# Gated delta attention and MLP on one core: keys and queries turned by VectorE and DMAs instead of TensorE

## The chip, the core and the metric

The kernel runs on one core of a Trainium2 chip. A core has TensorE (PE; PEld is its weight load), VectorE (DVE), ScalarE (ACT), GpSimd (POOL) and SyncE (SP), each with an instruction queue of its own that is worked off in order. Transfers are issued from the queues of SP and ScalarE. The metric is the device time of one execution in microseconds (us); less is better.

## What is computed

Cut from the reference: a delta-rule recurrence over 768 tokens in 32 heads (4 in the batch, 8 heads each, head size 48), and on its output an MLP with a hardswish.

```python
q, k, v: (4, 8, 768, 48); beta: (4, 8, 768); w_in: (384, 2048); w_out: (2048, 384)

k_n = k / (np.linalg.norm(k, axis=-1, keepdims=True) + 1e-06)
for t in range(S):
    y[:, :, t] = einsum('bhd,bhde->bhe', q[:, :, t], state)
    v_old = einsum('bhde,bhd->bhe', state, kt)
    state = state + bt[:, :, :, None] * einsum('bhd,bhe->bhde', kt, vt - v_old)
x = y.transpose(0, 2, 1, 3).reshape(3072, 384)
h = x @ w_in
out = (h * np.clip(h + 3.0, 0.0, 6.0) / 6.0) @ w_out
```

All is in float32.

## The kernel before

**Chunks and steps.** The 768 tokens of a sequence are cut into N = 24 chunks of C = 32. The 128 partitions of a tile hold 4 batch entries x 32 tokens of a chunk. Step t runs the chain of chunk t, and in the profile it begins with the product of keys and queries with the state (L806). A chunk needs, ahead of its step:

- `prep(t)`: GpSimd scales the keys to unit length (`kb`, L510); TensorE transposes keys and then queries, four 128x128 transposes each into a PSUM tile `pt` (L524); ScalarE copies each `pt` into a quarter of the tile `KQ`, which holds keys and queries with the head dimension on the partitions (L532); GpSimd makes a mask (`mb`, L486); TensorE multiplies keys with keys and queries (the scores `sc`, L547); VectorE masks these into `L` and `LB` (L558); GpSimd scales the keys by beta (`bkb`, L498).
- `inverse(g)`: for a group of four chunks (5 to 8, 9 to 12, 13 to 16, 17 to 20, 21 to 23) VectorE inverts the unit triangular matrices `L`, 30 rounds of a product (L759) and a difference (L764), between two block transposes of 128x1024 (L469, L473). The inverse of the next group is worked off during the present one, in pieces.

`chain(t)`, in order: L806 on TensorE; `R` from the values and the product with the state (L901, L909 on VectorE); `y` from the product with the queries (L843 on ScalarE, then L819 on VectorE); `pz`, the inverse times `R` (L827), which ScalarE copies out (L927); the new state (L938 on TensorE, L956 on VectorE); `py` (L827), added to `y` (L863); `y` transposed for the MLP (L873, copied by L877).

**MLP.** Two chunks make a block of 256 tokens. From block 5 on the up product is made by a scheme with eleven products instead of twelve: VectorE first makes sums of the tokens (`token_sums`, L1056); then for each of eight tiles TensorE begins (`begin`, L1066), ScalarE copies the first half of it (L1080), GpSimd forms sums (L1030), TensorE ends it (`end`), VectorE adds (L1093, L1097), ScalarE copies the rest, which empties the PSUM buffer (L1100), and makes the clipped part (L1104), and VectorE multiplies (L1107). Before block 5 the plain product stands there (L994, L1001 on ScalarE, L1004 on VectorE). From block 2 on the down product is made with seven half-size products (L1218); its sums are L1204 and L1228, ScalarE's copies L1225. The down product of one block runs in odd steps, the up product of the next in even steps. The result goes out from SP (`to_dram`, L1143): eight transfers of 48 KB near the end of each odd step.

**Order.** Every engine's order is written by hand. Up to step 4 a string lists each piece of work. From step LS = 5 on a loop has NU = 15 units a step. `plan` says which generator is advanced in which unit: `ch` is the chain, `now` the `prep` of the chunk whose products are made next, `later` the one after it; from step 7 on `now` is chunk t + 6. In every unit one piece of the MLP follows (`take(units)`), then pieces of the inverse, as many as a running sum allows (`room`, from constants for what VectorE has to do in that unit):

```python
room = max(1.65 - USED[mode["of"]] - CHAIN.get(u, 0), 0.15) / mode["mean"]
due += room * left / max((GS - i) * NU - u, 1)
```

In the kernel before, from step 7 on, `prep` scales the keys in unit 13, transposes keys in unit 1 of the next step and queries in unit 2, makes the scores in unit 4 and the masks in unit 5. The inverse starts in unit 6 of the second step of a group. `prep` of the last chunk, 23, ends in step 17.

**Buffers.** PSUM has a ring `pm` of four buffers, shared by `pt`, `pz`, `py`, the transposed `y` and the tiles of the MLP, and a ring `pc` of two for the state's products and the scores. `KQ` has six buffers, keys two (`kb`), queries four (`qb`). A query or key transfer has rows of 48 numbers (192 bytes), 256 rows in each.

Of the kernel before, what the change touches and what calls it, by code (L numbers as in the profile page):

```python
# [9 lines left out]
FP32 = mybir.dt.float32  # L10
# [34 lines left out]
def kernel(  # L45
# [34 lines left out]
    CB = 2  # L80
# [36 lines left out]
    mb_spare = spares[:, 8 * H * C : 10 * H * C]  # L117
    bkb_spare = spares[:, 10 * H * C : 10 * H * C + H * DP].rearrange("p (h w) -> p h w", w=DP)
    assert 10 * H * C + H * DP == 3 * NPR * P
    kbufs = [persist.tile([P, H, DP], FP32, name=f"kb{i}") for i in range(NKB)]  # L120
    qbufs = [persist.tile([P, H, DP], FP32, name=f"qb{i}") for i in range(NQB)]
    bkbufs = [bkb_spare] + [
        persist.tile([P, H, DP], FP32, name=f"bkb{i}") for i in range(1, NBKB)
    ]
# [12 lines left out]
    def needs(*what):  # L137
        assert past.issuperset(what), (what, set(what) - past)
# [33 lines left out]

    def load_q(t, eng=nc.sync):
        if t < N:
            if t >= NQB:
                needs(("qT", t - NQB))
            elif t:
                needs(*pad(t))
            for b in range(B):
                eng.dma_start(out=qbufs[t % NQB][rows(b), :, 0:D], in_=tokens(q, b, t))  # L180
                if b == B - 1:
                    past.add(("q", t))
                yield
# [310 lines left out]
    def scaled(t):  # L494
        needs(("kb", t), *pad(t), *([("bkb", t - NKB)] if t >= NKB else []))
        if t >= NBKB:
            needs(("su", t - NBKB + 1))
        nc.gpsimd.tensor_tensor(  # L498
            out=bkb_of(t)[:, :, 0:D], in0=kbufs[t % NKB][:, :, 0:D],
            in1=beta_tok[:, t, 0:H].unsqueeze(2).to_broadcast([P, H, D]), op=ALU.mult,  # L500
        )
        past.add(("bkb", t))
        yield

    def prep(t, whole=True):

        g, i = group(t)
        kb, qb = kbufs[t % NKB], qbufs[t % NQB]
        needs(*([("bkb", t - NKB)] if t >= NKB else []), *(pad(t) if t < NKB and t else []))
        nc.gpsimd.tensor_tensor(  # L510
            out=kb[:, :, 0:D], in0=kfs[g][:, i],
            in1=invs.pop(t).unsqueeze(2).to_broadcast([P, H, D]), op=ALU.mult,
        )
        past.add(("kb", t))
        yield

        for j, src in enumerate((kb, qb)):
            if j == 1:
                needs(("q", t))
                past.add(("qT", t))  # L520
            ring("pm", NPM, ("pt", t, j))
            pt = psM.tile([128, NP, P], FP32, name="pt", tag=slot["pm"])
            for p in range(NP):
                nc.tensor.transpose(  # L524
                    pt[:, p, :], src[:, 2 * p : 2 * p + 2].rearrange("p e w -> p (e w)"), ident[:]
                )
# [12 lines left out]
        ring("pc", NPC, ("sc", t))  # L539
        sc = psC.tile([P, 2, 512], FP32, name="sc", tag=slot["pc"])  # L540
        scv = sc[:, :, 0 : NP * 2 * C].rearrange("p e (a j w) -> p e a j w", a=NP, j=2)
        for p in range(NP):
            for b in range(B):
                for e in range(2):
                    r = slice(DP * e, DP * e + DP)
                    kq = KQ[r, p * B // 2 + b // 2]
                    nc.tensor.matmul(  # L547
                        scv[rows(b), e, p],
                        lhsT=kq[:, 3 if b % 2 else 0, :],
                        rhs=kq[:, 3:1:-1, :] if b % 2 else kq[:, 0:2, :],  # L550
                        start=True, stop=True,
                    )
        yield
        needs(*([("BZ", t - NLB)] if t >= NLB else []))
        LB = work.tile([P, H, C], FP32, name="LB", bufs=NLB)
        mb = mbs.pop(t)
        for j, out in enumerate((lowers(t), LB)):
# [229 lines left out]
    def chain(t, whole=True):  # L787
# [10 lines left out]
        def of_state():  # L798
            ph = [banks("ks", t, i) for i in range(2)]
            for p in range(NP):  # L800
                for b in (0, 2, 1, 3):
                    for e in range(2):
                        r = slice(DP * e, DP * e + DP)
# [622 lines left out]
    with tc.manual_schedule():  # L1426
# [11 lines left out]
        loads = iter(())  # L1438
        left = due = 0
        USED = {"up": 0.42, "eleven": 1.0, "down": 0.7}  # L1440
        CHAIN = {0: 0.45, 1: 0.75, 2: 0.75, 3: 0.4, 4: 0.4, 6: 0.5, 9: 0.8, 10: 0.6, 14: 0.2}
        for t in range(LS, N):
            g, i = group(t)
# [9 lines left out]
            if i == 2:  # L1453
# [12 lines left out]
                11: lambda: token_sums(t // CB),  # L1466
                13: lambda: take(later),
            }
            if behind:
                for u in (7, 8, 10, 11, 12, 13):  # L1470
                    plan[u] = lambda ch=plan.get(u): (ch and u < 13 and ch(), take(more))
                plan[14] = lambda: take(later)
            ready = (2, 0) if behind or i == 2 and t - LS == LA - LE else (1, 6)
            for u in range(NU):
                if u in plan:
                    plan[u]()
# [13 lines left out]
                settle(1)  # L1490
                while evicts:
                    evicts.pop(0)()
                if i == 1 == ready[0] and 5 < u < 7:
                    continue
                if i == 0 or not left:
                    take(fill, 2 if i or u < 2 else u > 4)
                    continue
                room = max(1.65 - USED[mode["of"]] - CHAIN.get(u, 0), 0.15) / mode["mean"]
                due += room * left / max((GS - i) * NU - u, 1)
                due = min(due, 2.6)  # L1500
                take(fill, int(due))
# [34 lines left out]
```

## Time and profile before

| | us |
|---|---|
| runs shown: median of 3 (lowest to highest) | 667.09 (667.01 to 669.37) |
| profiled execution | 672.08 |
| its span, first to last instruction | 670.4 |
| TensorE busy in the span | 636.9 |
| VectorE busy | 487.2 |
| ScalarE busy | 272.8 |
| GpSimd busy | 203.6 |

The granted clock of TensorE is 0.985 on average over the span, and 1.00 in every stretch from 130 us on. The profile is of one execution; a row gives line, engine, operation, tiles (out<-in) and shapes, count, busy time and the mean of one in ns, and then idle time of the engine just before it with what ended it. "SPq" and "ACTq" are transfers issued on these queues; "to landing" is the time from issue until the semaphore says that the data is there. Some steps: step 7 begins at 214.8 us, step 12 at 342.2, step 16 at 443.3, step 17 at 468.3, step 18 at 493.4.

### The profile page before, as it was taken

To read this page: it belongs to the slowest core of one execution; us is meant where nothing else is said; L and a number is where in the kernel's file an instruction comes from. 1 tells how busy PE (TensorE), PEld (TensorE's weight loads), DVE (VectorE), ACT (ScalarE), POOL (GpSimd) and SP (SyncE) were. 2 spreads that over 40 slices of the span, in tenths; PEclk is the share of its full clock that TensorE was granted. 3 is DMA by queue.
4 is the path that set the end of the run, shared out by engine and by line. 5 is a ranking of instruction groups with operands and counts; after the bars stand their busy time and mean duration, and the time that the engine had idled before them with its cause. 6 is when DMAs were issued, how large, how long until landed. Compare 5 with 4: busy or idle time off the path is not lost.

```text
span 670.4 us, 26330 instructions
## 1 busy us (share of the span) xinstructions
PE 636.9 (95%) x11544; PEld 568.6 (85%) x11544; DVE 487.2 (73%) x1146; ACT 272.8 (41%) x532; POOL 203.6 (30%) x320
## 2 busy tenths in 40 slices
PE   2768899999999999999999999999999999999997
PEld 2657786776688988988989999999999999999997
DVE  4889685899545777747879847988748988556354
ACT  5887568532142232232234234235244144153250
POOL 5531022002421031364155255055042141331330
PEclk9959899999999999999999999999999999999999
DMA  7888237302041030032030020020020020010000
GB/s 171 203 193 235 59 67 186 73 6 51 15 80 32 2 72 2 3 73 37 3 68 8 3 61 14 3 62 2 3 50 2 2 49 2 17 24 2 25 1 25
DMA packets 88499, 33.27 MB, mean 50 GB/s; under 512 B 80160, under 2 KB 83232, under 8 KB 88384
## 3 DMA queue, kind: packets, MB, share of 16 engines
q1 hardware_dynamic: 88128, 31.29, 20.7%
q8 instruction: 91, 1.49, 0.9%
q10 hardware_dynamic: 256, 0.30, 0.2%
q14 instruction: 24, 0.20, 0.1%
HBM read 26.84 MB, written 4.72 MB: 47 GB/s over the span
## 4 chain that ended last, share of the span: by engine, by line
PE 86%; DMA 5%; DVE 3%; SPq 2%; issue 1%; ACT 1%; POOL 0%; ACTq 0%; DVEq 0%; POOLq 0%
PE po L1218 28%; PE ph L1066 20%; PE ph L994 15%; PE po L1154 6%; PE ks L806 3%; PE su L938 3%; PE pz L827 3%; PE py L827 3%; PE pt L524 2%; PE sc L547 2%; DMA spare<-in_moe_w_in_dram 2%; DMA kf<-in_k_dram 1%; PE yt L873 1%; DMA w_out<-in_moe_w_in_dram 1%; PE pi L684 1%
## 5 line engine op out<-in xcount | busy, mean ns | idle before, releaser
L1066 PE MATMUL ph<-xT,w_in 128*128 128x128 f32 (+1 forms) x560 | 121.4, 321 | 0.8 <-ACT KQ L532 0.6
L994 PE MATMUL ph<-xT,w_in 128*128 128x256 f32 (+1 forms) x576 | 116.6, 351 | 2.9 <-DVE g L1004 2.1
L1218 PE MATMUL po<-w_out,g 128*128 128x192 f32 x640 | 110.6, 326 | 0.0
L994 PEld LDWEIGHTS ph<-xT,w_in 128*128 128x128 f32 x576 | 94.5, 192 | 15.8 <-DVE g L1004 2.9
L1218 PEld LDWEIGHTS po<-w_out,g 128*128 128x128 f32 x640 | 104.6, 190 | 0.5
L1066 PEld LDWEIGHTS ph<-xT,w_in 128*128 128x128 f32 x560 | 91.1, 191 | 6.0 <-ACT KQ L532 0.8
L1030 POOL TENSOR_TENSOR g<-g 128x256 f32<-128x256 f32 x112 | 68.0, 608 | 83.2 <-ACT g L1080 78.8
L1218 PE MATMUL po<-spare,g 128*128 128x192 f32 x480 | 86.7, 332 | 0.0
L1218 PEld LDWEIGHTS po<-spare,g 128*128 128x128 f32 x480 | 77.2, 190 | 1.8
L1001 ACT ACTIVATE g<-ph,halves 128x256 f32<-128x256 f32 (+1 forms) x96 | 41.3, 436 | 74.9 <-PE ph L994 74.8
L1080 ACT ACTIVATE g<-ph 128x512 f32<-128x512 f32 x56 | 33.4, 597 | 82.1 <-PE ph L1066 82.1
L1228 POOL TENSOR_TENSOR o<-o,u 128x192 f32<-128x192 f32 x18 | 13.2, 733 | 175.7 <-ACT o L1225 97.2
L1204 DVE TENSOR_TENSOR g<-g 128x512 f32<-128x512 f32 x80 | 55.6, 716 | 5.6 <-PE po L1218 5.6
L759 DVE TENSOR_TENSOR pr<-A 128x30 f32<-128x30 f32 (+9 forms) x150 | 57.4, 383 | 2.8
L764 DVE TENSOR_TENSOR A<-A,pr 128x30 f32<-128x30 f32 (+9 forms) x150 | 55.7, 371 | 3.7
L1004 DVE SCALAR_TENSOR_TENSOR g<-g,ph 128x256 f32<-128x256 f32 (+1 forms) x96 | 34.8, 371 | 31.7 <-ACT g L1001 31.4
L356 ACT ACTIVATE spare<-spare,places 128x768 uint16<-128x768 uint16 (+1 forms) x56 | 52.4, 942 | 2.7 <-DMA kf<-in_k_dram 1.5
L1093 DVE TENSOR_TENSOR g<-ph,g 128x256 f32<-128x256 f32 x56 | 23.5, 420 | 38.4 <-PE ph L1066 30.9
L1225 ACT ACTIVATE o<-po 128x192 f32<-128x192 f32 x40 | 13.2, 330 | 83.2 <-PE po L1218 79.6
L510 POOL TENSOR_TENSOR kb<-kf,inv 128x384 f32<-128x384 f32 x24 | 21.3, 891 | 78.8 <-issue 42.6
L1154 PE MATMUL po<-w_out,g 128*128 128x384 f32 x128 | 45.2, 491 | 0.0
L1107 DVE SCALAR_TENSOR_TENSOR g<-o,g 128x512 f32<-128x512 f32 x56 | 40.7, 726 | 5.9 <-ACT o L1104 5.9
(141 smaller groups left out, 1010.6 us busy)
## 6 DMA issues: line engine op xcount, KB each, us to landing
kf<-in_k_dram SPq DMA_DIRECT2D x96, 48.0 KB, 2.9
qb<-in_q_dram SPq DMA_DIRECT2D x96, 48.0 KB, 2.8
vf<-in_v_dram SPq DMA_DIRECT2D x96, 48.0 KB, 2.2
out_dram<-o SPq DMA_DIRECT2D x92, 48.0 KB, 1.6
spare<-in_moe_w_in_dram SPq DMA_DIRECT2D x4, 768.0 KB, 6.0
w_out<-in_moe_w_in_dram SPq DMA_DIRECT2D x4, 768.0 KB, 6.5
w_out<-in_moe_w_out_dram SPq DMA_DIRECT2D x4, 768.0 KB, 7.3
spare<-in_moe_w_out_dram SPq DMA_DIRECT2D x4, 768.0 KB, 5.7
```

The costliest lines, as they stand in the source:

```text
L356: nc.scalar.activation(out=z, in_=z if n else d.bitcast(I16)[:, :, :, 3], func=func, bias=places[:, n : n + 1], scale=scale,)
L759: nc.vector.tensor_tensor(out=pv, in0=A[:, j + 1 :, j].unsqueeze(2).to_broadcast([n, w, j]), in1=A[:, j, 0:j].unsqueeze(1).to_broadcast([n ...
L764: nc.vector.tensor_tensor(out=A[:, j + 1 :, 0:j], in0=A[:, j + 1 :, 0:j], in1=pv, op=ALU.subtract)
L827: nc.tensor.matmul(ps[rows(place(b)), D * h : D * h + D], lhsT=m(h)[rows(b)], rhs=z[rows(b), D * at(h) : D * at(h) + D], start=True, stop= ...
L994: nc.tensor.matmul(ph[:, cols], lhsT=w_in[:, s, f * 128 : (f + 1) * 128], rhs=xT[:, s, cols], start=(s == 0), stop=(s == NKT - 1),)
L1001: nc.scalar.activation(out=g, in_=ph, func=ACTF.Relu, bias=half, scale=1.0 / 6.0)
L1030: nc.gpsimd.tensor_tensor(out=out, in0=a, in1=b, op=op)
L1066: nc.tensor.matmul(ph[:, n], lhsT=w, rhs=x, start=start, stop=stop, skip_group_check=True)
L1107: nc.vector.scalar_tensor_tensor(out=g, in0=r, scalar=1.0, in1=g, op0=ALU.min, op1=ALU.mult)
L1154: nc.tensor.matmul(pos[c][:], lhsT=gs[blk, f // 2][:, f % 2, c * P : (c + 1) * P], rhs=w_out[:, f, :], start=(f == 0), stop=(f == NFC - 1),)
L1204: nc.vector.tensor_tensor(out=A(f, *out, 4), in0=A(f, *a, 4), in1=A(f, *b, 4), op=op)
L1218: nc.tensor.matmul(ps[n][:], lhsT=A(f - f % 2, *a)[:, f % 2], rhs=b[:, f], start=(f == 0), stop=(f == HF - 1),)
```

## The change

For chunks t >= TQ = 13 (prepared in steps 7 to 17) `prep` has no TensorE transposes and no ScalarE copies. VectorE turns the scaled keys, and then the queries, in blocks of 32x32 (one 128x384 instruction each) into `turned`, which lies in two of the former four query buffers. SP writes each half with four transfers into a DRAM tile `kq`, in rows of 32 numbers. When all eight are there, ScalarE issues two transfers that read `kq` into `KQ`. Scores and the products with the state then use 48 rows per head instead of 64. Keys and queries of these chunks are stored densely, and queries have two buffers.

The plan changes for these chunks: keys are scaled in unit 10, turned with their four writes in unit 11, queries with theirs in unit 12, the reads in unit 1 of the next step, scores in unit 6, masks in unit 7. The inverse starts in unit 8 instead of 6, and its pace leaves room for the turning in units 11 and 12.

```diff
+    TQ, HQ = LS + 2 * LE, 2
+    qb_pair = persist.tile([P, HQ, H, DP], FP32, name="qbs")
...
+    turned = qb_pair[:].rearrange("p i h w -> p (i h w)")[:, 0 : 2 * H * D].rearrange(
+        "p (k z) -> p k z", k=2
+    )
...
-        for j, src in enumerate((kb, qb)):
+        if t >= TQ:
+            kq = scratch.tile([H * D, B // 2, 4, C], FP32, name="kq", bufs=2)
+            for j, src in enumerate((of_key(t), of_query(t))):
+                if j == 1:
+                    needs(("q", t))
+                    past.add(("qT", t))
+                nc.vector.transpose(out=turned[:, j], in_=src.rearrange("p h w -> p (h w)"))
+                for b in range(B):
+                    nc.sync.dma_start(
+                        out=kq[:, b // 2, (3 if j == 0 else 2) if b % 2 else j, :].rearrange(
+                            "(n r) c -> r n c", r=C
+                        ),
+                        in_=turned[rows(b), j].rearrange("p (n c) -> p n c", c=C),
+                    )
+                yield
+            ring("KQ", NKQ, ("KQ", t))
+            KQ = work.tile([128, NP * B // 2, 4, C], FP32, name="KQ", bufs=NKQ)
+            for e in range(2):
+                nc.scalar.dma_start(
+                    out=KQ[DP * e : DP * e + D].rearrange("d (p x) y c -> d p (x y c)", p=NP),
+                    in_=kq[:].rearrange("(p e d) x y c -> e d p (x y c)", e=2, d=D)[e],
+                )
+            drain(mask(t))
+            yield
+        for j, src in enumerate((kb, qb) if t < TQ else ()):
...
+        TURN = {11: 0.75, 12: 0.75}
...
+            if first_of >= TQ:
+                plan[2] = lambda: (take(ch), take(gens["q"], 4))
+                plan[4] = lambda: take(ch)
+                plan[5] = lambda: None
+                plan[7] = lambda: take(now)
+            if first_of + 1 >= TQ and not behind:
+                plan[10] = lambda: (take(ch), take(later))
+                plan[11] = lambda: (token_sums(t // CB), take(later))
+                plan[12] = lambda: take(later)
+                plan[13] = lambda: None
...
-            ready = (2, 0) if behind or i == 2 and t - LS == LA - LE else (1, 6)
+            turns = TURN if first_of + 1 >= TQ else {}
+            by_dma = first_of >= TQ
+            ready = (2, 0) if behind or i == 2 and t - LS == LA - LE else (1, 8 if by_dma else 6)
...
-                room = max(1.65 - USED[mode["of"]] - CHAIN.get(u, 0), 0.15) / mode["mean"]
+                room = max(1.65 - USED[mode["of"]] - CHAIN.get({6: 7, 8: 6}.get(u, u) if by_dma else u, 0) - turns.get(u, 0), 0.15) / mode["mean"]
```

More of the change, by code (lines that the diff above doesn't have):

```diff
@@ L119, with of_key, of_query, dense @@
     assert 10 * H * C + H * DP == 3 * NPR * P
-    kbufs = [persist.tile([P, H, DP], FP32, name=f"kb{i}") for i in range(NKB)]
-    qbufs = [persist.tile([P, H, DP], FP32, name=f"qb{i}") for i in range(NQB)]
+    kbufs = [persist.tile([P, H, DP], FP32, name=f"kb{i}")[:] for i in range(NKB)]
+    TQ, HQ = LS + 2 * LE, 2
+    qb_pair = persist.tile([P, HQ, H, DP], FP32, name="qbs")
+    qbufs = [persist.tile([P, H, DP], FP32, name=f"qb{i}")[:] for i in range(NQB - HQ)] + [
+        qb_pair[:, i] for i in range(HQ)
+    ]
+    turned = qb_pair[:].rearrange("p i h w -> p (i h w)")[:, 0 : 2 * H * D].rearrange(
+        "p (k z) -> p k z", k=2
+    )
+    def of_key(t):
+        return dense(kbufs[t % NKB], t)
+    def of_query(t):
+        return dense(qbufs[t % NQB if t < TQ else t % (NQB - HQ)], t)
+    def dense(x, t):
+        if t < TQ:
+            return x[:, :, 0:D]
+        return x.rearrange("p h w -> p (h w)")[:, 0 : H * D].rearrange("p (h w) -> p h w", w=D)
+    def q_before(t):
+        slot = [s % NQB if s < TQ else s % (NQB - HQ) for s in range(t + 1)]
+        return max((s for s in range(t) if slot[s] == slot[t]), default=None)
     bkbufs = [bkb_spare] + [
@@ L174, in load_q @@
         if t < N:
-            if t >= NQB:
-                needs(("qT", t - NQB))
+            if q_before(t) is not None:
+                needs(("qT", q_before(t)))
             elif t:
@@ L179, in load_q @@
             for b in range(B):
-                eng.dma_start(out=qbufs[t % NQB][rows(b), :, 0:D], in_=tokens(q, b, t))
+                eng.dma_start(out=of_query(t)[rows(b)], in_=tokens(q, b, t))
                 if b == B - 1:
@@ L498, in scaled @@
         nc.gpsimd.tensor_tensor(
-            out=bkb_of(t)[:, :, 0:D], in0=kbufs[t % NKB][:, :, 0:D],
+            out=bkb_of(t)[:, :, 0:D], in0=of_key(t),
             in1=beta_tok[:, t, 0:H].unsqueeze(2).to_broadcast([P, H, D]), op=ALU.mult,
@@ L510, in prep @@
         nc.gpsimd.tensor_tensor(
-            out=kb[:, :, 0:D], in0=kfs[g][:, i],
+            out=of_key(t), in0=kfs[g][:, i],
             in1=invs.pop(t).unsqueeze(2).to_broadcast([P, H, D]), op=ALU.mult,
@@ L544, in prep @@
                 for e in range(2):
-                    r = slice(DP * e, DP * e + DP)
+                    r = slice(DP * e, DP * e + (DP if t < TQ else D))
                     kq = KQ[r, p * B // 2 + b // 2]
@@ L802, in of_state @@
                     for e in range(2):
-                        r = slice(DP * e, DP * e + DP)
+                        r = slice(DP * e, DP * e + (DP if t < TQ else D))
                         c = slice(2 * C * (b // 2), 2 * C * (b // 2) + 2 * C)
@@ L1472 @@
                 plan[14] = lambda: take(later)
-            ready = (2, 0) if behind or i == 2 and t - LS == LA - LE else (1, 6)
+                if first_of + 2 == TQ:
+                    plan[12] = plan[13] = lambda: (take(more), take(later))
+            turns = TURN if first_of + 1 >= TQ else {}
+            by_dma = first_of >= TQ
+            ready = (2, 0) if behind or i == 2 and t - LS == LA - LE else (1, 8 if by_dma else 6)
             for u in range(NU):
@@ L1492 @@
                     evicts.pop(0)()
-                if i == 1 == ready[0] and 5 < u < 7:
+                if i == 1 == ready[0] and u == ready[1]:
                     continue
```

## The prediction

> **What bounds the kernel now.** I read the page's busy shares and chain first, then the busy time by step, then the instructions in order of time in steps 15 to 17, then the groups by shape and the DMA queue.
>
> ```profile
> PE 636.9 (95%) x11544; PEld 568.6 (85%) x11544; DVE 487.2 (73%) x1146; ACT 272.8 (41%) x532; POOL 203.6 (30%) x320
> ...
> PE 86%; DMA 5%; DVE 3%; SPq 2%; issue 1%; ACT 1%; POOL 0%; ACTq 0%; DVEq 0%; POOLq 0%
> ```
>
> TensorE carries 86% of the chain that ends last. A step starts with its L806; the second table cuts the trace there (steps 15, 16, 17, then 19).
>
> ```profile
> core 0: us, PE busy (x) PEld busy (x) DVE busy (x) ACT busy (x) POOL busy (x), PEclk, DMA share, GB/s
> 418.20:443.30 25.10, 25.10 (x454) 23.87 (x453) 22.86 (x55) 6.10 (x13) 4.75 (x8) 1.00 0.05 12
> 443.30:468.30 25.00, 25.00 (x469) 22.81 (x468) 22.71 (x52) 12.73 (x26) 14.58 (x22) 1.00 0.16 33
> 468.30:493.40 25.10, 25.10 (x458) 23.87 (x457) 15.69 (x34) 6.21 (x13) 4.75 (x8) 1.00 0.05 12
> ...
> 516.50:539.90 23.40, 23.40 (x382) 22.33 (x381) 21.76 (x52) 4.30 (x10) 5.35 (x8) 1.00 0.05 13
> ```
>
> TensorE never rests. Step 17 is the last that prepares keys; step 19, the same work without that, is 1.7 us shorter although VectorE is busier. So TensorE sets the pace, and what leaves it shortens a step. VectorE, 91% busy in steps 15 and 16, is next in line.
>
> **What is removed.** Steps 7 to 17 prepare t = 13 to 23, each with two groups of four transposes (L524):
>
> ```profile
> 445.27 0.47 PEld L524 LDWEIGHTS pt<-ident,kb 128*128 128x128 f32 x4
> ...
> 445.70 0.30 PEld L1066 LDWEIGHTS ph<-xT,w_in 128*128 128x128 f32 x2
> ...
> 447.13 0.58 PEld L524 LDWEIGHTS pt<-ident,qb 128*128 128x128 f32 x4
> ...
> 447.68 0.30 PEld L1066 LDWEIGHTS ph<-xT,w_in 128*128 128x128 f32 x2
> ```
>
> Of the four lines, the second and fourth are the next work. From a group's first load to it: 0.43 and 0.55 us, mean 0.49. 22 groups make 10.8 us. One group in step 12 also holds TensorE for ScalarE's copy of it (waits for KQ L532, 0.8 us). **Gain 11.6 us.** The 0.86 us of L547 per step stays and moves from unit 4 to 6; 48 instead of 64 rows change no column count, so I cost that at nothing. ScalarE loses 22 copies of 0.6 us, off the path.
>
> [...]
>
> **What is added on VectorE.** 22 block transposes of 128x384. The rows on each side:
>
> ```profile
> L473 DVE STREAM_TRANSPOSE X<-A 128x1024 f32<-128x1024 f32 x6 | 11.9, 1984 | 0.2
> ...
> L694 DVE STREAM_TRANSPOSE sums_in<-X 128x256 f32<-128x256 f32 x4 | 1.7, 435 | 0.0
> ```
>
> By columns between them: 0.70 us, 1.4 a step. Besides, the new pacing moves inversion pairs (L759, L764) towards the end of their group: the built order has 24 such operations instead of 20 in step 16 (23 instead of 19 in step 12), and 5 instead of none in step 17 before L473. In steps 12 and 16 VectorE would need 22.7 + 1.4 + 1.3 = 25.4 us where TensorE would need 24.0. That alone costs about 1.5 us in each of the two, since L473's result is what L827 (pz) of steps 13 and 17 waits for. Steps 14 and 17 (17.96 and 15.69 of 25.1) cover theirs.
>
> **What is added in the queues.** Per step SP issues eight writes of 48 KB to DRAM, ScalarE two reads of 192 KB. The reads wait for all eight writes, and everything behind them on ScalarE waits too. So the question is when the last write lands, and where ScalarE then stands.
>
> After an even step SP has nothing else between the writes; they go out at units 11 and 12, and the reads stand at unit 1, some 7 us later: covered, to within about 0.5 us, and ScalarE is idle for 1.9 us just there. After an odd step the built order of SP is four key writes, eight output writes, four query writes. From the end of step 15 and the first half of step 16, in order of time on VectorE, ScalarE and SP's queue:
>
> ```profile
> 439.63 0.28 DVE L1056 TENSOR_TENSOR beta_tok<-xT,beta_tok 128x128 f32<-128x128 f32 x1
> ...
> 450.90 0.74 DVE L819 SCALAR_TENSOR_TENSOR y<-ks,parity,y 128x192 f32<-128x192 f32 x2 [0.39 <-ACT y L843]
> ```
>
> ```profile
> 446.37 0.72 ACT L1104 ACTIVATE o<-g,halves 128x512 f32<-128x512 f32 x1
> ...
> 449.37 0.27 ACT L1100 ACTIVATE g<-ph 128x128 f32<-128x128 f32 x1
> ...
> 450.30 0.56 ACT L843 ACTIVATE y<-ks,parity 128x384 f32<-128x384 f32 x1
> ```
>
> ```profile
> 198.85 7.28 SPq L168 DMA_DIRECT2D kf<-in_k_dram  x12
> ...
> 440.38 3.58 SPq L1143 DMA_DIRECT2D out_dram<-o  x8
> 444.01 1.90 SPq L193 DMA_DIRECT2D vf<-in_v_dram  x4
> ```
>
> The key transpose stands behind the token sums (L1056), which now end near 440.3 (one more inversion operation ahead): done at 441.0; the query one, behind one more operation, at 442.1. Key writes issue at 0.47 each (as the four vf) until 442.9, the outputs take 3.58 until 446.5, then the query writes start. Landing: the first as a kf load, 2.9 us after its issue. The writes have 384 packets each; twelve kf loads of 256 packets in a row took 7.28 us, 0.61 each, so I take 0.91 for each further one: last landing 446.5 + 2.9 + 2.7 = 452.1. The bounds: 450.1 if they keep up with the issue and land as vf does (2.2); well above 455 if short writes to DRAM are slow, which no row shows. I take 452.1, a load of nearly this size and shape being nearest.
>
> ScalarE reaches the reads after L1104, at 447.1. So it waits **5.0 us** (3.0 to 8 or more), plus two issues of 0.41 (the four output issues on its queue): free at 452.9 instead of 447.1. Behind the reads stand L1080, L1100, L1104, L843 and L927 of step 16. Who waits for them:
> - TensorE: the fifth tile of the block uses the buffer that L1100 empties. L1100 comes at 453.7 instead of 449.4; TensorE, done with pz at 450.2 (its R comes from VectorE), stands until 453.75 and reaches the sixth tile at 456.85 where 453.55 was possible: 3.3 us lost.
> - VectorE: L819 waits for L843 and starts 4.05 us late, with all that is queued behind it. In step 14 the 7 us of idle time cover this. In steps 12 and 16 they don't: carried through the order, y (L863) comes late for TensorE's L873, and L473 ends near 480.3 instead of 473.5; pz of step 17, possible at 475.6 - 1.5 = 474.2, starts then. 6.1 us lost, the first 3.3 and the 1.5 of VectorE in it.
>
> Steps 8 and 10 still run the plain up product. There are no token sums, the writes end by about 244.7, ScalarE comes at 243.6, and four buffers stand between it and TensorE: 1 us for both and for step 9.
>
> **Sum.** Steps 12 and 16 with their successors 2 x 6.1, step 14 3.3, steps 8 to 10 1.0: 16.5 us lost, 11.6 won. The profiled execution took 672.08 us (span 670.4): 677.0. The median of the runs is 667.09, a factor 0.9926: **672.0 us**. Each microsecond of ScalarE's wait counts three times, so no change would need a wait of 3.4 us.
>
> **Rivals.**
> *Faster: the writes land in time.* Place: the reads at unit 1 of steps 12, 14 and 16. If the query writes land 4 us earlier than I have it (wait up to 1 us), or if TensorE's buffers hide more, only VectorE's 1.5 us in two steps remain: 672.08 - 11.6 + 3 = 663.5, 658.6 as a median. It decides below a wait of about 2.2 us (over 0.5% faster). For it: issue to landing of single output writes is 1.6 us, and ScalarE is only 25 to 51% busy per step and can catch up. Against it: the issue alone lasts until 448.4, 1.3 us past ScalarE's arrival.
> *Much slower: short writes.* A write's rows are 128 bytes long; the shortest in the trace are the loads' 192 bytes. In the built order a transfer waits for the eighth before it, so the last output write waits for the last key write. If a write takes double of what I took (1.8 us), that one lands at 441.0 + 2.9 + 5.4 = 449.3 and the last query write near 458: a wait of 11 us, six more than taken, 18 us more for the three steps and some in the others: 672.0 + 18 = 690. [...]
> *No change.* A wait between 2.2 and 4.5 us gives 663.8 to 670.4.
>
> **Chances.** This kernel's measurement tells about 0.5% from no change. Slower by ScalarE's wait: 0.42, own range 670.4 to 681. Slow writes: 0.10, 681 and up. Faster: 0.34, 656 to 663.8. Between: 0.14. The forecast is the first, 672.0. From 657 to 686, 0.07 of the slow end and about as much of the fast end are left out. So 0.34 faster, 0.14 within, 0.52 slower.
>
> **What the profile will show.** Right: L524 has 104 instead of 192 weight loads; 22 new 128x384 transposes near 0.7 us; in steps 12, 14 and 16 an idle time of ScalarE of about 5 us before L1080, ended by a DMA, and TensorE idle there; VectorE's L819 waiting 4 us; pz of steps 13 and 17 waiting for L473. Wrong: if ScalarE's idle time there is under 2 us, the writes were quicker than I sized them; if it is 5 us and TensorE does not rest, the buffers cover more than I traced.

## The result, and the profile after

The changed kernel took **689.61 us** (median of 4 runs, 686.59 to 693.17) against 668.14 for the kernel before (4 runs): a ratio of 1.0323, 95% interval 1.0267 to 1.0379. Slower, as forecast, but by 21 us where 5 were forecast, and outside the range given. In two of the experiments one run took over 1.5% longer than the fastest of its kernel (689.86 us with SP's reads, 692.12 with three faults mended); medians and ratios are given without it.

The profiled execution took 693.17 us, span 691.4, mean granted clock 0.961. Lines have moved by 46, those of the inverse by 22: L1066 of the prediction is L1112 here, L1080 is L1126, L1100 is L1146, L1104 is L1150, L843 is L889, L819 is L865, L827 is L873, L901 and L909 are L947 and L955, L938 is L984, L547 and L558 are L593 and L604, L473 is L495, L806 is L852. New are L545 (VectorE's transposes), L547 (SP's writes) and L557 (ScalarE's reads).

The page's busy shares, and its chain:

```profile
PE 641.1 (93%) x11456; PEld 569.5 (82%) x11456; DVE 497.5 (72%) x1168; ACT 259.3 (37%) x510; POOL 201.5 (29%) x320
...
PE 79%; DVE 10%; ACT 3%; issue 3%; DMA 2%; SPq 2%; ACTq 0%; POOL 0%; DVEq 0%
```

88 weight loads are gone, yet TensorE is busy 4 us longer and carries 79% of the chain instead of 86%; VectorE's part rose from 3% to 10%. The cause of both shows in the table by step (steps 15, 16, 17, then 19):

```profile
core 0: us, PE busy (x) PEld busy (x) DVE busy (x) ACT busy (x) POOL busy (x), PEclk, DMA share, GB/s
426.60:451.00 24.40, 24.40 (x446) 23.00 (x445) 22.92 (x54) 4.36 (x11) 6.91 (x11) 1.00 0.27 47
451.00:480.70 29.70, 25.99 (x458) 23.63 (x457) 23.52 (x55) 11.53 (x24) 12.67 (x20) 0.94 0.31 58
480.70:509.60 28.90, 26.21 (x450) 24.72 (x449) 17.49 (x41) 5.11 (x12) 5.54 (x9) 0.94 0.20 38
532.70:556.10 23.40, 23.40 (x382) 22.33 (x381) 19.76 (x50) 4.30 (x10) 5.15 (x8) 1.00 0.05 12
```

Step 15 is 0.7 us shorter than before. Step 16 is 4.7 longer: TensorE now rests 3.7 us, and PEclk is 0.94. Before, every step had 1.00 there. Cut finer around the first of these places:

```profile
core 0: us, PE busy (x) PEld busy (x) DVE busy (x) ACT busy (x) POOL busy (x), PEclk, DMA share, GB/s
456.66:460.07 3.41, 1.45 (x67) 0.94 (x65) 1.85 (x4) 1.16 (x3) 0.00 (x0) 1.00 0.57 94
460.07:463.49 3.42, 3.10 (x14) 3.11 (x15) 1.87 (x5) 2.69 (x7) 1.49 (x3) 0.50 1.09 184
463.49:466.90 3.41, 3.41 (x84) 2.94 (x83) 3.31 (x8) 1.16 (x2) 1.18 (x2) 1.00 0.00 0
```

TensorE was busy for 1.45 of 3.41 us, and then got half the clock for 3.42 us, in which it did 14 matmuls where the next stretch has 84 (of other, partly shorter kinds). The profile shows five such periods after 90 us, at 357.7 (6.8 us), 381.6, 460.1, 490.8 and 589.8 us (3.4 each): 20.5 us at half speed, at most half of that, 10.2 us, lost. The kernel before has none between 76 us and the last 0.3 us of its span, when its matmuls are over.

What put TensorE to rest at 456.7 is in the order of time on ScalarE, in SP's queue, on VectorE and on TensorE:

```profile
453.79 0.27 ACT L1146 ACTIVATE g<-ph 128x128 f32<-128x128 f32 x1
456.60 0.72 ACT L1150 ACTIVATE o<-g,halves 128x512 f32<-128x512 f32 x1 [2.54 <-DMA out_dram<-o]
458.71 0.81 ACTq L557 DMA_DIRECT2D KQ<-kq  x2
459.57 0.60 ACT L1126 ACTIVATE g<-ph 128x512 f32<-128x512 f32 x1 [2.25 <-DMA kq<-qbs]
```

```profile
448.77 1.86 SPq L547 DMA_DIRECT2D kq<-qbs  x4
450.73 4.51 SPq L1189 DMA_DIRECT2D out_dram<-o  x8
455.35 1.92 SPq L547 DMA_DIRECT2D kq<-qbs  x4
```

```profile
457.36 0.69 DVE L1153 SCALAR_TENSOR_TENSOR g<-o,g 128x512 f32<-128x512 f32 x1 [1.67 <-ACT o L1150]
457.96 0.40 DVE L810 TENSOR_TENSOR A<-A,pr 128x240 f32<-128x240 f32 x1
458.28 0.61 DVE L955 SCALAR_TENSOR_TENSOR R<-ks,parity,R 128x384 f32<-128x384 f32 x1
```

```profile
459.04 0.88 PE L873 MATMUL pz<-R,X 32*32 32x48 f32 x64 [1.82 <-DVE R L955]
460.39 0.80 PE L1112 MATMUL ph<-xT,w_in 128*128 128x128 f32 x2 [0.46 <-ACT g L1146]
```

The order is the forecast one: key writes, outputs, query writes. But ScalarE waits twice. First L1150, the last instruction ahead of the reads, waits 2.54 us for an output transfer, since it writes into the buffer `o` of the last block, whose outputs now stand behind the key writes. Then 2.25 us pass before L1126: 1.4 until the query writes have landed and 0.8 to issue the two reads. TensorE rests twice too. Its pz waits 1.82 us for `R`, which stands on VectorE behind L1153, and that waits for L1150: this is the wait for the outputs. Then it waits 0.46 us for L1146, which stands behind the reads. By these lines either wait of ScalarE alone stops TensorE here, that for the outputs until 459.0, that for the reads until 460.4. Who waits on TensorE, over the whole span:

```profile
PE pz L873 <- DVE X L495: 7.3, 4, 2.7
...
PE su L984 <- DVE LB L604: 4.3, 2, 2.9
PE pz L873 <- DVE R L955: 4.3, 3, 1.8
```

The four waits for `X` (the inverse) are in steps 9 (0.7), 13 (2.0), 17 (2.7) and 21 (1.9). Before, the only wait of TensorE from step 7 on above 0.2 us was 0.6 us. The second line was in no part of the prediction: the product of the new state (L984) waits, in steps 12 and 16, for the masks of the scores of the chunk that is being prepared.

The new instructions themselves were no dearer than forecast. VectorE's transposes, and two rows of the transfers (KB each, median us from issue to landing):

```profile
L545 DVE STREAM_TRANSPOSE qbs<-kb x11: 522/567/579, 210.9 to 477.2; 128x384 f32<-128x384 f32 x11
L545 DVE STREAM_TRANSPOSE qbs<-qb x11: 555/571/579, 212.0 to 479.2; 128x384 f32<-128x384 f32 x11
```

```profile
out_dram<-o SPq DMA_DIRECT2D x92, 48.0 KB, 1.6
kq<-qbs SPq DMA_DIRECT2D x88, 48.0 KB, 1.8
```

### The profile page after: what moved, and what is told of

Read it like the earlier page. It is cut to its first block, busy times and chain, and to the rows that moved or that the text cites. A ratio compares the mean times of both kernels' runs of the same rounds, so it can differ in the third digit from the quotient of the medians.

```text
span 691.4 us, 26278 instructions
## 1 busy us (share of the span) xinstructions
PE 641.1 (93%) x11456; PEld 569.5 (82%) x11456; DVE 497.5 (72%) x1168; ACT 259.3 (37%) x510; POOL 201.5 (29%) x320
## 3 DMA queue, kind: packets, MB, share of 16 engines
q1 hardware_dynamic: 123328, 35.62, 25.4%
## 4 chain that ended last, share of the span: by engine, by line
PE 79%; DVE 10%; ACT 3%; issue 3%; DMA 2%; SPq 2%; ACTq 0%; POOL 0%; DVEq 0%
PE po L1264 24%; PE ph L1040 16%; PE ph L1112 15%; PE po L1200 6%; PE su L984 3%; PE ks L852 3%; PE py L873 3%; PE sc L593 2%; PE pz L873 2%; PE pt L570 2%; ACT spare L378 2%; DVE pr L805 2%; DVE X L495 1%; DVE A L810 1%; PE yt L919 1%
## 5 line engine op out<-in xcount | busy, mean ns | idle before, releaser
L1112 PE MATMUL ph<-xT,w_in 128*128 128x128 f32 (+1 forms) x560 | 123.5, 325 | 1.6 <-ACT g L1146 1.6
L1040 PEld LDWEIGHTS ph<-xT,w_in 128*128 128x128 f32 x576 | 95.8, 195 | 13.1 <-ACT xT L923 0.8
L1112 PEld LDWEIGHTS ph<-xT,w_in 128*128 128x128 f32 x560 | 93.0, 195 | 7.3 <-ACT g L1146 2.0
L1264 PE MATMUL po<-spare,g 128*128 128x192 f32 x480 | 91.0, 345 | 0.5 <-issue 0.5
L1264 PEld LDWEIGHTS po<-spare,g 128*128 128x128 f32 x480 | 82.3, 200 | 2.5 <-issue 0.8
L1126 ACT ACTIVATE g<-ph 128x512 f32<-128x512 f32 x56 | 33.4, 597 | 89.6 <-PE ph L1112 81.1
L1153 DVE SCALAR_TENSOR_TENSOR g<-o,g 128x512 f32<-128x512 f32 x56 | 39.7, 709 | 10.4 <-ACT o L1150 10.3
L1150 ACT ACTIVATE o<-g,halves 128x512 f32<-128x512 f32 x56 | 40.4, 722 | 16.2 <-DMA out_dram<-o 7.8
```

Of the source, the lines that this page charges most:

```text
L1040: nc.tensor.matmul(ph[:, cols], lhsT=w_in[:, s, f * 128 : (f + 1) * 128], rhs=xT[:, s, cols], start=(s == 0), stop=(s == NKT - 1),)
L1112: nc.tensor.matmul(ph[:, n], lhsT=w, rhs=x, start=start, stop=stop, skip_group_check=True)
L1150: nc.scalar.activation(out=r, in_=g, func=ACTF.Relu, bias=half, scale=1.0 / 6.0)
L1153: nc.vector.scalar_tensor_tensor(out=g, in0=r, scalar=1.0, in1=g, op0=ALU.min, op1=ALU.mult)
L1264: nc.tensor.matmul(ps[n][:], lhsT=A(f - f % 2, *a)[:, f % 2], rhs=b[:, f], start=(f == 0), stop=(f == HF - 1),)
```

## The experiments

The first three steps, some 125 us, differ from run to run (step 7 begins at 208.5 to 217.1 us in the profiles, with the same work ahead of it), so the totals of one kernel scatter by some us. I therefore also compare steps: length of a step in the profile of a run less its length before, in us, from the first weight load of the state's product to the next one. Each column is one execution; that of the changed kernel is the slowest of its four, that with SP's reads the fastest of its own. Steps 18, 19 and 22 differ in none of these. The last row leaves out the start of the span.

| step | after | e1 SP reads | e3 late scores | e5 late inverse | e7 all three | e8 odd | e9 early | e11 six |
|---|---|---|---|---|---|---|---|---|
| 7 | -0.68 | -0.33 | +0.20 | 0 | -0.45 | +0.57 | +1.40 | 0 |
| 8 | -0.68 | -0.68 | +1.15 | 0 | +0.76 | 0 | -0.88 | -0.88 |
| 9 | +0.11 | +0.12 | +0.19 | 0 | +0.12 | -0.64 | +0.21 | +0.46 |
| 10 | -0.68 | -0.48 | +0.19 | 0 | +3.03 | 0 | -0.88 | -0.88 |
| 11 | +0.34 | +0.35 | +0.24 | 0 | +0.90 | -0.88 | -0.88 | -0.88 |
| 12 | +6.75 | +1.64 | +3.06 | +0.42 | +3.30 | +0.26 | -0.73 | -1.31 |
| 13 | +3.07 | +1.53 | +0.60 | +0.41 | +3.08 | 0 | +0.61 | 0 |
| 14 | +1.38 | +1.89 | +0.05 | +0.24 | +1.70 | -0.21 | -1.12 | -1.14 |
| 15 | -0.68 | -0.68 | +0.19 | 0 | -0.68 | -0.88 | -0.79 | -0.88 |
| 16 | +4.73 | +2.60 | +1.53 | +0.71 | +2.11 | +0.91 | +1.38 | +0.22 |
| 17 | +3.75 | +2.07 | +0.84 | +0.68 | +2.08 | 0 | +4.97 | +0.39 |
| 20 | +1.26 | +1.36 | +1.13 | +0.97 | 0 | 0 | 0 | 0 |
| 21 | +3.64 | +1.98 | +0.46 | +0.47 | 0 | 0 | 0 | 0 |
| sum | +22.3 | +11.4 | +9.8 | +3.9 | +15.9 | -0.9 | +3.3 | -4.9 |
| half clock, us | 20.5 | 0 | 0 | 0 | 10.2 | 0 | 6.8 | 0 |

**Reads issued by SP.** The changed kernel, with one word different:

```diff
-                nc.scalar.dma_start(
+                nc.sync.dma_start(
                     out=KQ[DP * e : DP * e + D]...
```

> The changed kernel, but SP issues the two reads of the DRAM tile instead of ScalarE, at the same place. Theory A (ScalarE's queue: it stands first for the output writes, then for the key and query writes, about 2.2 us of the latter in steps 12, 14 and 16, and TensorE, starved by it, then runs at half clock for 3.4 us): ScalarE no longer has an idle time ended by kq<-qbs, steps 12 and 16 become 3 to 4 us shorter each, step 14 1.5 us; 680 to 684 us. Rival B (VectorE has more work than it can do in steps 12 and 16): those steps keep their length within 1 us, 687 to 690 us. Rival C (moving the scores and the pace of the inverse, not the transfers): 687 to 690 us.

Measured: 677.88 us median of three (676.96 to 684.64), ratio 1.0155 (1.0062 to 1.0247) against 667.09. Half of the loss is gone, by the medians and by steps: the difference from the changed kernel is 22.3 - 11.4 = 10.9 us, and this profile has no half clock after 46 us where the other has 20.5 us of it, worth up to 10.2. TensorE still rests in steps 16 and 17:

```profile
440.30:467.90 27.60, 24.53 (x462) 22.12 (x461) 23.64 (x55) 11.50 (x24) 12.15 (x20) 1.00 0.34 62
467.90:495.00 27.10, 24.41 (x446) 23.00 (x445) 17.44 (x41) 5.06 (x12) 5.47 (x9) 1.00 0.20 40
```

27.60 - 24.53 = 3.1 us and 27.10 - 24.41 = 2.7 us of rest (3.7 and 2.7 in the changed kernel), but at full clock. The waits left in these two steps:

```profile
PE pz L873 <- DVE X L495: 2.7, 1, 2.7
ACT o L1150 <- DMA out_dram<-o: 2.7, 1, 2.7
PE pz L873 <- DVE R L955: 2.5, 1, 2.5
```

So theory A is right on the queue, and only in part on the price. The wait for L1146 is gone, and so is that for the masks (4.3 us in steps 12 and 16 together). The wait for the outputs is not: L1150 still waits 2.7 us for one, and pz for `R` 2.5 us in each of these steps. And not all of the 10.9 us is the work of the reads. In steps 13, 17 and 21 TensorE waits for `X` as long as in the changed kernel (2.1, 2.7 and 1.9 us against 2.0, 2.7 and 1.9), yet they are 1.5, 1.7 and 1.7 us shorter, since no stretch at half clock follows here. That is a price of such a stretch, 1.5 to 1.7 us; and 4.9 of the 10.9 us come from the clock alone, at waits that moving the reads did not change.

**Pace as before where nothing is turned.** In steps 18 to 23 nothing is turned, but the new pace and the late start hold there too (the flags ask only for a chunk number of at least 13).

```diff
-            turns = TURN if first_of + 1 >= TQ else {}
-            by_dma = first_of >= TQ
+            turns = TURN if TQ <= first_of + 1 < N else {}
+            by_dma = TQ <= first_of < N
```

> The changed kernel, with the late start and slower pace of the inverse confined to steps in which keys are still prepared (so not in steps 18 to 20). Theory A and rival C: steps 20 and 21, which were 1.3 and 3.6 us longer than before, go back to within 0.3 us of before, with no half clock in step 21; 684 to 686 us. Rival B (VectorE's added transposes alone): no turning is in steps 18 to 21, so nothing changes by its mechanism; 689 us, and steps 20 and 21 stay long for a reason still to be found.

Measured: 691.19 us (688.16 to 692.64), ratio 1.0318 (1.0251 to 1.0386). Steps 20 and 21 differ by 0.00 us from before, as theory A and rival C have it, so their 4.9 us came from the pace and the late start alone. The total did not fall to the 684 to 686 expected: this profile has 23.9 us of half clock instead of 20.5, and steps 12, 16 and 17 are 0.9, 1.0 and 1.3 us longer than in the changed kernel. Where the clock falls moves from run to run, and such a run hides a gain of this size.

**Late scores and late inverse alone.** The kernel before, its transposes on TensorE, with the scores in unit 6, the masks in unit 7 and the inverse from unit 8:

```diff
+            if first_of >= LS + 2 * LE:
+                plan[4] = lambda: take(ch)
+                plan[5] = lambda: None
+                plan[7] = lambda: take(now)
+            by_dma = first_of >= LS + 2 * LE
...
-            ready = ... else (1, 6)
+            ready = ... else (1, 8 if by_dma else 6)
```

> The kernel before, with TensorE's transposes and ScalarE's copies as they were, but scores in unit 6, masks in unit 7 and the inverse from unit 8 on, in all steps from 7 on. Theory A: the scores in a run of their own cost TensorE 0.3 us in eleven steps (the eleven transposing steps gained 0.68 instead of the 0.98 us that the transposes take), and the late inverse costs steps 13, 17 and 21 1 to 3.6 us each: 675 to 680 us. Rival C: most of the loss is here, 685 us or more. Rival B: 668 to 671 us.

Measured: 679.50 us (678.24 to 682.01), ratio 1.0143 (1.0068 to 1.0219): 12 us lost with nothing turned at all, 9.8 by the steps of the profile. The steps that lose are of three kinds. Those without any wait lose 0.2 (7, 9 to 11, 15): the scores now stand in a run of their own. In steps 12 and 16 TensorE waits 1.2 us each for the masks (step 12 has two more waits, 0.7 us for a copy of `KQ` and 1.2 that the profile puts down to nothing, and step 8 one of 0.7 of that kind). VectorE and then TensorE in step 12:

```profile
359.15 0.48 DVE L759 TENSOR_TENSOR pr<-A 128x184 f32<-128x184 f32 x1
359.56 0.41 DVE L558 TENSOR_TENSOR L<-sc,mb 128x256 f32<-128x256 f32 x1
359.89 0.41 DVE L558 TENSOR_TENSOR LB<-sc,mb 128x256 f32<-128x256 f32 x1
```

```profile
355.51 0.86 PE L547 MATMUL sc<-KQ 64*32 64x64 f32 x64
358.92 0.32 PE L938 MATMUL su<-R,bkb 32*64 32x48 f32 x4
360.45 0.84 PE L938 MATMUL su<-R,bkb 32*64 32x48 f32 x60 [1.21 <-DVE LB L558]
```

The scores end at 356.4, but their masks come only at 359.6, behind inversion operations, and until then one of the two buffers of the ring `pc` is taken; L938 needs it after four of its matmuls. In the kernel before, step 12 has the scores in unit 4, the masks end at 354.0 and L938 starts at 356.7. The third kind, 13, 17, 20 and 21, is in the main the late inverse, as the next run shows. Theory A's range holds this total.

**Late inverse alone.** Scores left in unit 4, only the start moved:

```diff
-            ready = ... else (1, 6)
+            ready = ... else (1, 8 if first_of >= LS + 2 * LE else 6)
```

> The kernel before, with its transposes on TensorE and its scores in unit 4, and only the start of the inverse moved from unit 6 to unit 8 of the second step of a group, for the groups whose last chunk is prepared in steps 10, 14 and 18. It splits the 12 us that the late scores and the late inverse cost together (679.5 against 667.1). Theory A, the late inverse: VectorE has two units less for the same 30 rounds, so X (L473) comes late for steps 13, 17 and 21; in the earlier run the steps 12, 13, 16, 17, 20 and 21 carried 7.6 us of the loss, and they should carry it here too: 673 to 676, pz waiting for X or R there. Rival B, the late scores: a product of the scores in a run of its own holds a buffer of the ring pc and breaks up TensorE's stream, so this kernel, whose scores stay, is no slower: 666 to 669.

Measured: 671.63 us (669.42 to 676.02) against 669.07, ratio 1.0026 (0.9991 to 1.0061): by totals no difference that can be told; by steps 3.9 us, in the forecast places (12, 13, 16, 17, 20, 21, and 0.24 in 14). Theory A has the places, and half of the 7.6 us that it put there; the late scores, or the two together, are the larger part, 9.8 - 3.9 = 5.9 us.

**A rest of TensorE by itself.** The kernel before, with needless fills on VectorE ahead of `R` in steps where nothing is turned:

```diff
+            for _ in range({18: 2, 20: 4, 22: 6, 23: 8}.get(t, 0)):
+                nc.vector.memset(qbufs[0][:], 0.0)
```

> The kernel before, with 2, 4, 6 and 8 memsets of 128x512 on VectorE ahead of R in steps 18, 20, 22 and 23, so that TensorE stands before pz for a growing time. If a rest of TensorE lowers its granted clock: half clock for 3.4 us after the rests of about 2 us and more, none after the one under 1 us, and such a step grows by its rest and 1.7 us more. If the half clock in the changed kernel comes from elsewhere: clock 1.00 throughout, steps longer by the rest alone.

Measured: 672.34 us, one run. The cover in these steps was larger than I had allowed for: TensorE rested at most 1.66 us (step 20), and pz behind that took 0.88 us, as without a rest in step 18. This run tells nothing of longer rests. With more fills, `{18: 8, 20: 9, 22: 12}`:

> The kernel before with needless fills of 128x512 on VectorE (0.485 us each) ahead of R in steps 18 (8 of them), 20 (9) and 22 (12), where nothing is turned; the output is the same. It measures a rest of TensorE by itself. In the traces so far the clock falls to a half for the next 3.41 us whenever TensorE's matmuls leave 1.9 us or more of one stretch of 3.413 us empty (ten of ten such stretches in the changed kernel and in the second run; none of those with 1.73 us or less; two borderline ones at 1.91 and 1.98 us in the first run kept the full clock). Theory A, the empty share of a stretch decides: steps 20 and 22 get rests of about 4 us, so at least one stretch holds 2 us of each, and a stretch of 3.4 us at half clock follows each, costing 1.7 us beyond the rest; step 18, with a rest of 1.5 to 2.5 us, only if it falls into one stretch. Total some 672 + 8 + 3.4 = 680 to 685. Rival B, the drops in the changed kernel came from something else in it, its DMAs for example: no drop here, and steps 20 and 22 lose the rests alone.

Measured: 692.73 us, one run, and the clock fell after all three rests. Step 18 first, then step 20:

```profile
500.45:503.87 3.42, 1.05 (x66) 0.94 (x66) 2.59 (x7) 1.50 (x4) 0.46 (x1) 1.00 0.31 54
503.87:507.28 3.41, 3.41 (x16) 3.32 (x17) 1.64 (x5) 1.95 (x4) 0.81 (x2) 0.50 0.05 11
...
551.65:555.07 3.42, 0.00 (x0) 0.00 (x0) 3.01 (x8) 0.28 (x1) 0.00 (x0) 1.00 0.01 1
555.07:558.48 3.41, 2.53 (x69) 2.44 (x70) 2.87 (x8) 1.68 (x3) 0.00 (x0) 0.50 0.31 61
558.48:561.89 3.41, 3.41 (x15) 3.14 (x15) 0.77 (x3) 1.49 (x3) 1.18 (x2) 0.50 0.00 0
561.89:565.31 3.42, 3.42 (x84) 3.01 (x82) 2.87 (x7) 1.49 (x3) 1.19 (x2) 1.00 0.00 0
```

Nothing but the fills differs from before, so the rest alone does it: rival B is out. Steps 18, 20 and 22 lost 4.08, 7.63 and 7.95 us, 19.7 together; pz waited 2.37, 4.79 and 5.00 us in them, 12.2 together, and the other 7.5 us are the clock's, with 17.1 us at half of it. The total came out above what was expected, since the rests were longer (12.2 us instead of 8), and since two of the three brought two stretches at half clock, not one.

**Three faults mended at once.** Reads on SP, the pace as in the second experiment, and after odd steps the outputs ahead of the writes:

```diff
+                if t % CB:
+                    plan[11] = lambda: token_sums(t // CB)
+                    plan[13] = lambda: take(later)
```

> The changed kernel with three faults mended: the reads are issued by SP, the pace of the inverse goes back to that of before for steps 18 to 23 in which nothing is turned, and after odd steps keys are turned in unit 12 and queries in unit 13, so that SP issues the eight outputs before the eight writes. Theory A: what was left with SP's reads (681.3) were waits of pz for R, since ScalarE's L1150 waited 2.7 us for an output that stood behind the key writes (2.5 us in each of steps 12 and 16, 1 us in step 14), waits for X (2.1, 2.7 and 1.9 us) and steps 20 and 21 (3.3 us). With outputs first the waits for R go, with the pace back steps 20 and 21 are as before: 671 to 674. Rival B: the writes now land later, so that the scores wait for the keys instead: 677 to 682.

Measured: 681.26 us median of five (680.91 to 688.35), ratio 1.0189 (1.0130 to 1.0248): rival B. TensorE's waits in its profile:

```profile
PE sc L593 <- DMA KQ<-kq: 8.9, 8, 2.1
...
PE pz L873 <- DVE X L495: 5.6, 3, 2.7
```

The waits of pz for `R` fell from 6.2 us (SP's reads alone) to 1.2, as theory A has it, but the scores now wait 8.9 us for `KQ`. At this place in an odd step one queue has outputs and writes to issue, and in these two runs whichever went second was late: an output by 2.7 us for L1150 with SP's reads, `KQ` by up to 2.1 us for the scores here.

**The odd chunks alone.** Chunks 13, 15, 17 and 21, turned where SP issues no outputs, scores and inverse as before:

```diff
+    TURNED = (TQ, TQ + 2, TQ + 4, TQ + 8)
...
-        if t >= TQ:
+        if t in TURNED:
             kq = scratch.tile(...)
...
+            by_dma = False
```

> The change for the chunks 13, 15, 17 and 21 alone: those turned in steps 6, 8, 10 and 14, after which SP issues no outputs and in which VectorE is not the busiest, and read back in steps 7, 9, 11 and 15. The others keep the transposes of before; scores stay in unit 4, the inverse starts in unit 6. Theory A: TensorE loses 8 groups of four transposes at 0.49 us, and nothing waits, since the inverse, the outputs and ScalarE's second half of the order stay as they were: 667.1 - 3.9 = 663.2 (662 to 665). Rival B: the reads land only after unit 4 of the odd steps (issued in unit 1, 3.8 us to landing), so that TensorE waits for KQ and may rest for over 1.9 us in a stretch: 667 to 675.

Measured: 668.63 us (666.95 to 670.50) against 669.07, ratio 0.9993 (0.9966 to 1.0019): no difference, within rival B's range. Steps 9, 11 and 15 won 0.64, 0.88 and 0.88, near the 0.98 forecast; step 7 lost 0.57, its scores waiting 0.7 us for KQ, and step 16 lost 0.91. With chunk 13 left out and the pace of before:

> As the run with the odd chunks alone, with chunk 13 left on TensorE too, and the pace of the inverse of before: chunks 15, 17 and 21 turned, and read back in steps 9, 11 and 15. In the earlier run these steps won 0.64, 0.88 and 0.88 us, while step 7 lost 0.57 (scores waiting for KQ) and step 16 lost 0.91. Theory A: step 16's loss came from the pace, which held back inversion operations in step 14 for the turning and pushed them into steps 15 and 16: without it step 16 is as before, and the whole is 2.4 us faster than before (0.4%). Rival B: step 16's loss came from the turning in step 14 itself: step 16 still loses 0.9, 1.5 us faster than before (0.2%).

Measured: 670.98 us (668.38 to 675.58) against 669.68, ratio 1.0021 (0.9990 to 1.0052): no difference. Theory A fell: step 16 still lost 0.73. Rival B has that step, but not its 1.5 us of gain. In this profile step 15 lost 2.55: its scores waited 0.8 us for KQ and 0.7 us more behind ScalarE, and a half clock of 3.4 us followed.

**All eleven turned, but early.** Keys and queries turned in units 7 and 8, so that all writes are issued ahead of the outputs; reads in unit 0; scores, masks and the start of the inverse where they stood before (its pace leaves 0.6 us for the turning in each of units 7 and 8):

```diff
             if first_of >= TQ:
+                plan[0] = lambda: (take(ch), take(now))
+                plan[1] = lambda: take(ch)
                 plan[2] = lambda: (take(ch), take(gens["q"], 4))
...
+                plan[6] = lambda: (take(now), take(later))
+                plan[7] = lambda: take(later)
+                plan[8] = lambda: (take(ch), take(later))
                 plan[13] = lambda: None
...
+            by_dma = False
```

> All eleven chunks turned by VectorE and DMAs as in the changed kernel, but at another place in the step: keys scaled in unit 6, turned in unit 7, queries in unit 8, so that all eight writes are issued ahead of the outputs of an odd step; the reads in unit 0 of the next step instead of 1; scores and masks back in units 4 and 5, and the inverse from unit 6 with the pace of before (less 0.6 us in units 7 and 8). Theory A: the loss of the change lies in its places, all of it: writes behind outputs, scores in a run of their own, a late inverse, and the half clock that the rests of TensorE brought. With these gone 22 groups x 0.49 = 10.8 us are won, less what VectorE's 1.14 us a step costs in steps 12 and 16 (22.7 + 1.1 = 23.8 of 24.0, so 0 to 3 us): 658 to 662. Rival B: the turning itself doesn't fit: the outputs, now behind the writes, hold up ScalarE's L1150 and with it R, or the scores wait for KQ by 0.5 to 1 us a step as in the odd steps of the earlier run: 665 to 672, and 680 if a rest brings the half clock again.

Measured: 673.90 us (669.13 to 678.29) against 669.68, ratio 1.0048 (1.0013 to 1.0082). Six steps (8, 10, 11, 12, 14, 15) won 0.73 to 1.12 us each; 7, 9, 13, 16 and 17 lost 8.6, and up to 3.4 of that is the clock, after a wait of 2.07 us of pz for X in step 17. In steps 13 and 16 pz waited 1.4 us for `R`, in step 9 1.0 for X, and in step 7 the scores 2.0 for KQ. Neither theory's number, but it shows which steps can carry the turning. That VectorE's share of it (1.14 us a step) is what makes X late near the end of an inverse is likely, but not shown by itself.

**Those six.** Chunks 14, 16, 17, 18, 20 and 21 of the same kernel; the others stay on TensorE.

> The run with all eleven chunks turned early, cut to the six chunks whose steps won there: 14, 16, 17, 18, 20 and 21 (turned in steps 7, 9, 10, 11, 13 and 14, read back in steps 8, 10, 11, 12, 14 and 15); the others keep TensorE's transposes. In that run the steps 8, 10, 11, 12, 14 and 15 were 0.73 to 1.12 us shorter each, while 7 (scores waiting for KQ), 13, 16 and 17 (X late for VectorE's share of the turning) lost 8.4 us, 3.4 of them through half a clock. Theory A: without the turning in steps 8, 12, 15 and 16 the inverse ends as before, and the six gains of 0.88 us stay: 5.3 us faster, 664 (0.8%). Rival B: the inverse of the chunks 17 to 20, worked off from step 14 on beside one more turning, still ends late for step 17: 666 to 670, no difference that the runs can tell.

Measured: **663.42 us** (660.55 to 669.35) against 667.55, ratio 0.9951 (0.9924 to 0.9978): theory A, half a per cent faster than the kernel before. By steps it wins 4.9 us, 0.88 or more in each of the six, with 1.1 us given back in 9, 16 and 17. TensorE's part of the chain is 84%, and its profile has no half clock after 83 us.

## Why the prediction was wrong, step by step

**The gain, 0.98 us a step: right, a little large.** Where nothing else changed, a step without its two groups of transposes won 0.88 (ten steps of the last four kernels). So TensorE had no slack there. In the changed kernel it won 0.68, since the scores' run of its own took 0.2 back.

**VectorE: right in the main.** A transpose took 0.57, not 0.70, and VectorE was busy 23.5 us in step 16, where 25.4 were added up. X came late for steps 13 and 17 all the same: pz waited 2.0 and 2.7 us for it, 4.7 together, where the forecast has 2 x (6.1 - 3.3) = 5.6. With early turning, where the late start and the late scores are gone, step 17 still waited 2.1 us for X, but step 13 did not.

**The queues: the wait was there, and something smaller.** ScalarE stood 2.54 + 2.25 = 4.8 us ahead of L1126, where 5.8 were forecast (5.0 of wait and 0.8 of issues). Not seen was that half of it is a wait for the *outputs*: the prediction moved the query writes past the outputs, but didn't ask what the key writes ahead of the outputs do to the buffer `o`. Since the query writes landed only at 458.7, this wait made the reads no later; but it stops TensorE by itself, as the run with SP's reads shows. Where TensorE stands for the tiles, 3.3 us were forecast in each of steps 12, 14 and 16; it rested 1.9, 1.7 and 2.3 us there (`R` and L1146 together), 5.9 instead of 9.9. VectorE's L865 waited up to 2.9 us, not 4.

The rival with slow short writes gave 690 us, almost the measured number, and is wrong; that it came nearest was luck. That a short write takes double was the author's assumption, and no run shows it: a write of 48 KB in rows of 128 bytes landed in 1.8 us, 0.2 later than an output of 48 KB (1.6).

**The failed steps.** The sum gave +4.9 us; the steps 7 to 22 show +22.3. The missing 17.4:

- *A rest of TensorE was priced at its own length.* The prediction counted 3.3 and 6.1 us where TensorE stands, and no more. Five times the clock then fell to a half: 20.5 us, six stretches, up to **10.2 us** (9.2 at the lowest price measured, 1.54 each). This is the largest part, and in the filled kernel it followed three rests of 2.37, 4.79 and 5.00 us, with nothing else changed. Of the five drops three follow a wait for X (steps 13, 17 and 21), one the wait for the masks (step 12), and one the rest for the outputs and the reads in step 16.
- *"48 instead of 64 rows change no column count, so I cost that at nothing"*, of the scores moved from unit 4 to 6. The products themselves cost the same: a median of 216 ns each with 64 rows (L547 before) and with 48 (L593 after, from 210 us on). What changed was their neighbours. Late scores and inverse alone cost **9.8 us** by steps in a kernel that turns nothing; in the changed kernel steps 20 and 21 lost 3.2 (4.9 less 1.7 of clock; pace and late start, by the second experiment), where the prediction had no term at all, and steps 7 to 11 won 1.6 us together instead of 3.9 (2.3 less: 0.2 a step by the scores' run of its own, 0.7 by a wait for X in step 9; the rest is not divided).
- The remaining 1.7 us lie in steps 12 to 17: measured 19.0, less 8.5 of clock is 10.5, against 8.8 in the sum. The rests there add up to 14.9 us, where 15.5 were forecast, and the gain in these six steps was 14.9 - 10.5 = 4.4 instead of 6.7. That the rests agree so well is luck: the tiles had 5.9 instead of 9.9 us, X 4.7 instead of 5.6, and the masks 4.3 instead of nothing.

10.2 + 3.2 + 2.3 + 1.7 = 17.4.

**The clock.** The five drops in the profile of the changed kernel begin 7, 23, 9 and 29 times 3.413 us apart, so stretches of that length are read here, by the matmul records (their ends are modelled). Ahead of these five the stretch had 1.91, 1.96, 2.00, 2.57 and 2.60 us without a matmul. In the filled kernel it had 2.37 (step 18; TensorE was busy for 1.05 us of it) and 3.42 (step 20), with early turning 2.07 (step 17). In two more runs, first SP's reads, then three faults mended:

```profile
445.07:448.48 3.41, 1.43 (x10) 0.98 (x8) 1.73 (x3) 2.31 (x5) 1.72 (x4) 1.00 0.54 88
448.48:451.90 3.42, 2.93 (x81) 2.85 (x82) 3.32 (x10) 1.63 (x5) 0.38 (x2) 1.00 0.85 166
...
302.78:306.19 3.41, 1.93 (x68) 1.63 (x69) 1.14 (x3) 0.28 (x1) 0.00 (x0) 1.00 0.54 67
306.19:309.61 3.42, 3.42 (x10) 2.38 (x8) 1.72 (x3) 0.47 (x1) 3.25 (x5) 0.50 0.00 0
```

1.98 us without a matmul kept the clock, and 1.48 us did not; in the changed kernel 1.68 us (405.46 to 408.88) kept it. So these records give no single length of rest that parts the two, and why is open. Nor does the length of a wait say it: in step 17 pz waited 2.7 us for X both in the changed kernel, where PEclk of the step is 0.94, and with SP's reads, where it is 1.00. The clock was at half for 3.4 us after 1.91, 1.96, 2.00, 2.37 and 2.60 us, and for 6.8 us after 2.07, 2.57 and 3.42; what decides between these was not shown.

## What to carry to other kernels

Where TensorE sets the pace without rest, price each wait in front of it twice: its length, and what the clock does after it; here waits of 1.9 to 2.7 us (for X in steps 13, 17 and 21) cost 1.5 to 1.7 us more where a stretch at half clock followed. A product that is only moved holds its PSUM buffer until its reader comes (with the late scores L938 waited 1.21 us for that in step 12), so look up where that reader stands in the other engine's order before calling the move free. And a change that wins a little in every step and loses much in a few should be made only in those that have room: six of eleven chunks were faster than none and than all.

## What the runs showed of the hardware that was not expected

The granted clock was 0.50 for 3.42 us after a stretch of 3.41 us with 1.48 us without a matmul (three faults mended), and stayed at 1.00 after one with 1.98 us (SP's reads). A stretch at half clock cost 1.5 to 1.7 us where it could be read off alone (steps 13, 17 and 21, the changed kernel against SP's reads). TensorE was also at half for 6.8 us in a row: in step 20 of the filled kernel, after a stretch that was wholly empty, although TensorE worked 2.53 us in the first 3.41 of these; and in step 12 of the changed kernel after 2.57 us of rest. And 48 KB written to DRAM in rows of 128 bytes landed in 1.8 us (median of 88), 48 KB of output in 1.6.
